# Whole-row loads for the first batch's values, one tile for a group's turned probabilities, uncut products, and a plan with other lengths, in a kernel of banded attention and a gated layer

## The chip, the cores and the metric

The kernel runs on one core of a Trainium2 chip. The metric is the device time of one execution in microseconds (us), the median over several runs. The core's engines are TensorE (PE, the matrix multiplies; the loading of its weights is shown apart, as PEld), VectorE (DVE), ScalarE (ACT), GpSimd (POOL) and SyncE (SP, which here issues the loads from memory). Each engine takes its own instructions strictly in the order in which they were written.

## The reference

```python
# q, k, v: 8 batches x 8 heads x 576 positions x 64; heads 0-3 see the last 32 positions,
# heads 4-7 every fourth of the last 128
scores = scale * np.matmul(q, k.transpose(0, 1, 3, 2))
scores = np.where(masks[None, :, :, :], scores, -1000000000.0)
attn = softmax(scores)                             # written out in the reference
x = heads_side_by_side(np.matmul(attn, v))         # 576 x 512 a batch
h = np.maximum(x @ w_in, 0.0)                      # w_in 512 x 1024
u, v = (h[..., :d_ff // 2], h[..., d_ff // 2:])
v_n = (v - mu) / np.sqrt(var + 1e-06)              # mean and variance over the 512 of a row
v_s = np.einsum('ts,bsd->btd', w_spatial, v_n) + b_spatial[None, :, None]
out = (u * v_s) @ w_out                            # w_out 512 x 512
```

## The kernel before

**Tiles.** The eight heads of a batch are four pairs, and two pairs make a group (`G` = 0 near heads, 1 far heads). The 576 positions are 18 blocks of 32. A block of queries sees 64 keys, its own 32 and the 32 before, and so scores, probabilities and products are many small matmuls, each on a part of TensorE's array. A group's scores come in three units of six blocks (`unit`), each with a maximum, exponentials, a sum, a division on POOL, and a transposition on DVE (L867) that writes the turned probabilities into a tile `pT` of a third of a group. There are four such tiles. `weighted` multiplies a group's values with them, after all three units, into four banks of accumulators: for each block of 32 keys one matmul over the two blocks of queries that see it, 64 columns, but two matmuls of 32 columns where these two lie in different units and so in different tiles. `evacuated` copies the products out and `features_in` splits each pair's into a high and a low part, the features `x` of the layer behind.

Matmuls run at a reduced format, and so every factor is split in two: a copy on ACT (`hi`) and a difference (`lo`), on DVE through `sub` (L537), or by a short fold on TensorE (L600 to L602 for a weight, L651 and L652 for a spatial one) and a copy. A weight's way begins with ACT's first step (L585) and DVE's steps L587, L591 and L594. The gated layer has `v_tile` (the second half of `h`, L973), `upper` (the first half, batch 0), `gate` (the spatial product, L1093) and `piece` (the products with `w_out`, and from batch 1 on those with the first half of `w_in`, as seven products in place of eight, L1281, with sums and differences of factors: `factor`, `joined`).

**Loads.** All loads of keys, values and weights are issued by SyncE into eleven tiles `kqv` of 128 x 1152 numbers. A load takes the tile that its plan gives it and waits on the chip until what stood there has been read. For batch 0 the list `LOADS` sets their order: `kq0` is the keys and queries of a pair (`kq0a` its first third, `kq0b` the rest), `v0` the values of a group, `wi12` a slice of `w_in`, `wo0` of `w_out`, `sp4` of the spatial weights. In memory a key's row holds the 18 blocks' values of both heads of the pair, 4608 bytes in one piece.

**Order.** A planner (`Timeline`) runs while the program is built. Every step is a strand that says, before each part, which engine it needs, for how many microseconds, and which tiles. The planner takes the strand that could start first, corrected by a rank, and writes its instructions. The ranks come from tables (`SHIFT`, `SECOND`, `FIRST`, `RANKS`); the microseconds stand in the code. The chip then keeps this order on each engine, whatever the real lengths. Until 30 us of the plan TensorE's gaps are filled with matmuls on zeros (L1401).

Of the kernel before, what the change touches and what calls it, by code (L numbers as in the profile page):

```python
# [26 lines left out]
    ('differences', 0): 0.468,  # L27
    ('differences', 1): 6.175,
    ('factor', 0): -7.854,
    ('factor', 1): 3.191,  # L30
    ('factor', 10): -9.348,
    ('factor', 11): -10.686,
    ('factor', 12): -7.566,
    ('factor', 13): -0.364,
    ('factor', 14): -3.99,
    ('factor', 2): -2.237,
    ('factor', 3): 1.347,
    ('factor', 4): -5.468,
    ('factor', 5): -2.002,
    ('factor', 6): 0.064,  # L40
    ('factor', 7): 3.683,
    ('factor', 8): -4.426,
    ('factor', 9): 11.423,
    ('features_in', 0): -1.929,
    ('features_in', 1): -6.483,
    ('features_in', 2): 1.799,
    ('features_in', 3): 2.762,
    ('gate', 0): 0.195,
    ('gate', 1): 0.043,
    ('gate', 2): -0.747,  # L50
    ('gate', 3): 3.234,
    ('gate', 4): -0.329,
    ('gate', 5): -3.407,
    ('gate', 6): -5.019,
    ('gate', 7): -2.472,
    ('heads_in', 0): -18.264,
    ('heads_in', 1): -7.458,
    ('heads_in', 2): -11.465,
    ('heads_in', 3): -5.984,
    ('piece', 0): -5.965,  # L60
    ('piece', 1): -2.471,
    ('piece', 10): 1.261,
    ('piece', 11): -3.149,
    ('piece', 12): -0.447,
    ('piece', 13): -1.085,
    ('piece', 14): 0.115,
    ('piece', 15): -6.645,
    ('piece', 16): -3.48,
    ('piece', 17): 0.704,
    ('piece', 18): -3.672,  # L70
    ('piece', 19): -3.913,
    ('piece', 2): -3.945,
    ('piece', 20): 0.716,
    ('piece', 21): 0.502,
    ('piece', 22): -5.774,
    ('piece', 23): -1.128,
    ('piece', 24): -2.828,
    ('piece', 25): -2.689,
    ('piece', 26): 0.874,
    ('piece', 27): 2.135,  # L80
    ('piece', 3): -2.111,
    ('piece', 4): -2.378,
    ('piece', 5): 1.404,
    ('piece', 6): -1.667,
    ('piece', 7): -0.342,
    ('piece', 8): -2.98,
    ('piece', 9): -6.786,
    ('unit', 0): 0.628,
    ('unit', 1): 0.566,
    ('unit', 2): 1.826,  # L90
    ('unit', 3): 0.588,
    ('unit', 4): 0.52,
    ('unit', 5): 0.142,
# [313 lines left out]
def tile_banded_attention_gated_moe(  # L407
# [25 lines left out]
    D = 64  # L433
# [1150 lines left out]
```

## Time and profile before

| | |
|---|---|
| device time, median of 3 runs | 551.05 us (550.04 to 551.29) |
| the profiled execution | 551.94 us, of which its span is 550.2 us |
| TensorE busy | 527.7 us, 7836 instructions |
| DVE busy | 385.4 us, 878 instructions |
| ACT busy | 360.1 us, 970 instructions |
| POOL busy | 194.2 us, 226 instructions |
| moved by DMA | 46.72 MB, mean 85 GB/s |

The span is that of one execution, from its first instruction to its last. Busy times are sums over the whole span, in which stages with different limits follow each other, so what one stage waits for is read from that stage.

### The profile page before, as it was taken

The numbers are of one execution on the slowest core, as the hardware profiler recorded it, in microseconds if no ns is written. First come the engines' busy times: TensorE is split into PE (matmuls) and PEld (weight loads), VectorE is DVE, ScalarE is ACT, GpSimd is POOL, SyncE is SP. The second block draws the span as 40 slices with busy tenths as digits, with TensorE's granted clock in tenths as the row PEclk, the third lists the DMA queues.
The fourth block names the chain that finished last, engine by engine and source line by source line (L and its number), as shares of the span: only waits on it lengthen the run. The fifth ranks groups of instructions, "written<-read, shape, count | busy, mean of one in ns | idle before, by whom it ended". The sixth has DMA issues, their size and how long they took to land.

```text
span 550.2 us, 18561 instructions
## 1 busy us (share of the span) xinstructions
PE 527.7 (96%) x7836; PEld 478.2 (87%) x7836; DVE 385.4 (70%) x878; ACT 360.1 (65%) x970; POOL 194.2 (35%) x226
## 2 busy tenths in 40 slices
PE   9989999995999999999999998899999998999997
PEld 6766798884999979889999998889999998989996
DVE  6864979998867758677669675577758674666554
ACT  4787986756785568745785757746686666646423
POOL 3410337354324522265216341365216440253000
PEclk9998999997999999999999999999999998999999
DMA  8784423203344123221253014221252010001002
GB/s 273 190 306 151 128 69 108 89 4 84 112 130 109 53 79 88 61 72 55 67 143 89 19 60 131 71 72 54 55 142 60 11 66 4 13 0 59 29 1 87
DMA packets 60455, 46.72 MB, mean 85 GB/s; under 512 B 41298, under 2 KB 50514, under 8 KB 60372
## 3 DMA queue, kind: packets, MB, share of 16 engines
q1 hardware_dynamic: 60372, 45.54, 28.2%
q8 instruction: 61, 1.00, 0.8%
q14 instruction: 22, 0.18, 0.1%
HBM read 36.08 MB, written 9.44 MB: 83 GB/s over the span
## 4 chain that ended last, share of the span: by engine, by line
PE 76%; DVE 9%; ACT 6%; DMA 5%; issue 2%; SPq 1%; POOL 0%; DVEq 0%; ACTq 0%
PE bank L1281 31%; PE bank L1093 16%; PE bank L973 12%; PE bank L897 6%; PE bank L797 4%; PE bank L993 2%; DMA kqv<-in_w_in_dram 2%; DMA kqv<-in_w_out_dram 2%; ACT raw L929 2%; PE bank L1073 1%; PE bank L1072 1%; SPq L772 1%; DMA kqv<-in_kT_dram 1%; PE bank L1060 1%; DVE x L537 1%
## 5 line engine op out<-in xcount | busy, mean ns | idle before, releaser
L1093 PE MATMUL bank<-wt,fac 128*128 128x288 f32 x768 | 114.3, 297 | 1.4 <-ACT x L944 1.1
L1093 PEld LDWEIGHTS bank<-wt,fac 128*128 128x128 f32 x768 | 106.6, 189 | 3.2 <-ACT x L944 1.3
L862 POOL TENSOR_TENSOR p<-p,rv 128x384 f32<-128x384 f32 x48 | 42.6, 888 | 123.6 <-DVE rv L860 122.0
L973 PE MATMUL bank<-wih,x 128*128 128x512 f32 x256 | 84.9, 394 | 0.2 <-DVE x L537 0.2
L839 ACT ACTIVATE p<-p,nm 128x64 f32<-128x64 f32 x180 | 60.4, 337 | 10.9 <-DVE nm L833 10.8
L1367 ACT COPY ur<-bank 128x288 f32<-128x288 f32 x120 | 45.7, 397 | 32.4 <-PE bank L1281 28.9
L929 ACT COPY raw<-bank 64x288 f32<-64x288 f32 (+1 forms) x96 | 49.7, 541 | 16.0 <-PE bank L897 14.7
L973 PEld LDWEIGHTS bank<-wih,x 128*128 128x128 f32 x256 | 48.0, 188 | 10.4 <-DVE x L537 0.6
L537 DVE TENSOR_TENSOR fac<-ur,fac 128x576 fp32r<-128x576 f32 x56 | 47.3, 859 | 10.2 <-ACT fac L1210 10.2
L1281 PE MATMUL bank<-fac,woh 128*128 128x288 f32 x256 | 54.1, 302 | 0.0
L1018 POOL TENSOR_TENSOR rs<-rs,halfneg 128x1 f32<-128x1 f32 (+1 forms) x40 | 28.4, 710 | 68.5 <-DVE rs L1015 68.2
L1267 POOL TENSOR_TENSOR raw<-raw,raw 128x576 f32<-128x576 f32 x21 | 33.8, 1608 | 51.6 <-DVE fac L537 40.1
L1210 ACT CAST fac<-ur 128x576 fp32r<-128x576 f32 x56 | 36.7, 673 | 22.9 <-POOL ur L1267 12.5
L1281 PE MATMUL bank<-fac,o 128*128 128x288 f32 x288 | 44.7, 302 | 6.2 <-ACT ur L1367 6.0
L973 PE MATMUL bank<-wil,x 128*128 128x512 f32 x128 | 50.2, 392 | 0.0
L1344 DVE TENSOR_TENSOR ur<-ur,bank 128x288 f32<-128x288 f32 x90 | 39.2, 448 | 14.6 <-PE bank L1281 10.0
L1281 PEld LDWEIGHTS bank<-fac,o 128*128 128x128 f32 x288 | 41.3, 194 | 7.3 <-ACT ur L1367 6.5
L1267 POOL TENSOR_TENSOR ur<-ur,ur 128x576 f32<-128x576 f32 x28 | 41.3, 1475 | 11.8 <-DVE fac L537 8.1
L1281 PEld LDWEIGHTS bank<-fac,woh 128*128 128x128 f32 x256 | 42.8, 193 | 1.9
L897 PE MATMUL bank<-pT,kqv 32*64 32x64 f32 (+1 forms) x2688 | 34.8, 229 | 8.0 <-issue 7.2
L797 PEld LDWEIGHTS bank<-kqv 64*32 64x32 f32 x2304 | 34.8, 119 | 7.3 <-issue 5.9
L897 PEld LDWEIGHTS bank<-pT,kqv 32*64 32x64 f32 x2688 | 32.1, 130 | 10.2 <-issue 8.9
(157 smaller groups left out, 1143.7 us busy)
## 6 DMA issues: line engine op xcount, KB each, us to landing
kqv<-in_vw_dram SPq DMA_DIRECT2D x128, 72.0 KB, 2.6
out_dram<-ur SPq DMA_DIRECT2D x64, 144.0 KB, 1.7
kqv<-in_kT_dram SPq DMA_DIRECT2D x30, 288.0 KB, 3.2
kqv<-in_qT_dram SPq DMA_DIRECT2D x30, 288.0 KB, 4.5
kqv<-in_w_in_dram SPq DMA_DIRECT2D x8, 512.0 KB, 6.7
kqv<-in_w_out_dram SPq DMA_DIRECT2D x4, 512.0 KB
kqv<-in_w_spT_dram SPq DMA_DIRECT2D x5, 288.0 KB, 2.9
kqv<-in_kT_dram SPq DMA_DIRECT2D x2, 192.0 KB, 3.8
```

The lines of the kernel that those rows point to most:

```text
L537: nc.vector.tensor_sub(out, a, b.bitcast(F32))
L797: nc.tensor.matmul(s[w][q * QB : q * QB + QB, e, :], kq[r, :S].rearrange("p (u n i t) -> p u t n i", n=2, i=QB, t=US)[:, (u + places[b, pa ...
L839: nc.scalar.activation(p[:, e, j], s[j][:, e] if first else p[:, e, j], AF.Exp, bias=nm[:, i : i + 1], scale=SCALE if first else 1.0, accu ...
L862: nc.gpsimd.tensor_mul(flat, flat, spread_out(rv))
L897: nc.tensor.matmul(acc[h][i][1][1][col : col + D, o : o + len(run) * QB], v[r, c * D : c * D + D], probs[b, G, u][1][r, at : at + len(run) ...
L929: nc.scalar.copy(dst[to], src[at])
L973: nc.tensor.matmul(pm, x[a][:, cols], wi[w][:, c, NF:], start=c == 0 and n == 0, stop=c == NC - 1 and n == 2)
L1093: nc.tensor.matmul(pv, left[:, a, i, m * P : m * P + P], wt[:, k, h, w, i], start=n == 0, stop=False, skip_group_check=True)
L1267: (eng.tensor_add if kind == "s" and n == 1 else eng.tensor_sub)(at(to), at(left), at(right))
L1281: nc.tensor.matmul(bank[:, :HS], lhs, rhs, start=fresh and n == 0, stop=n == 5, skip_group_check=not fresh or kind == "s")
L1344: nc.vector.tensor_add(ob[1][:, m], ob[1][:, m], bank[:, :HS])
L1367: nc.scalar.copy(ob[1][:, m], bank[:, :HS])
```

## The change

Values of batch 0: a group takes two `kqv` tiles, one for the 32 keys that stand before a block and one for the block's own, and each of its eight loads brings 32 whole rows of 4608 bytes, with both heads of the pair, of which a row's place in the tile uses one. Before, a load brought one head's 18 pieces of 256 bytes from each row, side by side with the other kind's. Later batches load as before. Probabilities: the three transpositions of a group write parts of one tile, of which there are two; the first of them takes the tile, and the others wait until it has. Products: no matmul is cut at a unit's border any more (76 instead of 84 calls a group; the profile counts two instructions for each). The table of masks has 18 places instead of 24, and `minus` has a tile of its own. The planner's lengths for some steps are raised, and the tables of ranks and the list of loads have other numbers throughout.

```diff
-    ('weighted', 0): -3.76,
-    ('weighted', 1): -3.947,
+    ('weighted', 0): -2.858,
+    ('weighted', 1): 1.375,
...
-sp4 kq1b wi00 wi12 kq0a kq0b kq1a kq2 wi11 kq3 wi10 wo0 v0 v1 sp3 wi03 wi02 sp2 sp1 wi13 wi01 wo3 wo1 sp0 wo2
-bias
+kq1a wi11 wi00 wi10 kq0a kq3 wi12 sp1 wi01 bias kq2 kq1b v0 wi13 wi02 wo0 kq0b sp3 v1 sp4 sp2 wo1 wi03 wo3 sp0
+wo2
...
-KNOBS = {'wide': (1, (1, 2)), 'plain': (8, (1, 2))}
+KNOBS = {'apart': 2, 'wide': (1, (1, 2)), 'plain': (8, (1, 2))}
...
-            pT=bufs("pT", [P, 2 * US * KW], 4),
+            pT=bufs("pT", [P, NB * KW], 2),
...
-    masks = const.tile([P, 2 * US + NB, KW], BF16, name="masks")
+    masks = const.tile([P, NB, KW], BF16, name="masks")
...
+        apart = b == 0 and G < KNOBS["apart"]
         yield turn("v", b, G)
-        yield "kqv"
-        (big,) = yield DMA, 4.2, 2.0
-        for i, n in itertools.product(range(2), range(2)):
-            src = vw[b, 2 * G + i, (n + 1) * QB : (n + 2) * QB].rearrange("k (t j d) -> j k t d", j=2, d=D)
-            for j in range(2):
-                to = (2 * i + j) * QB
-                nc.sync.dma_start(big[1][to : to + QB, :BIG].rearrange("p (t n d) -> p t n d", n=2, d=D)[:, :, n, :], src[j])
-        taken("v", b, G, 6.2)
-        values[b, G] = big
+        yield "kqv kqv" if apart else "kqv"
+        got = values[b, G] = yield DMA, 3.8 if apart else 4.8, 2.0
+        for i, n, j in itertools.product(range(2), range(2), range(2)):
+            r = slice((2 * i + j) * QB, (2 * i + j + 1) * QB)
+            src = vw[b, 2 * G + i, (n + 1) * QB : (n + 2) * QB]
+            if apart:
+                nc.sync.dma_start(got[n][1][r], src)
+            else:
+                dst = got[0][1][r].rearrange("p (t n d) -> p t n d", n=2, d=D)
+                nc.sync.dma_start(dst[:, :, n, :], src.rearrange("k (t j d) -> j k t d", j=2, d=D)[j])
+        taken("v", b, G, 5.8 if apart else 6.8)
...
-        *held, pb = yield PE, 0.77 if first else 0.68, 0.0
+        *held, pb = yield PE, 0.8 if first else 0.71, 0.0
...
-        yield "pT"
-        (probs[n],) = yield DVE, 0.5, 0.08
-        nc.vector.transpose(probs[n][1], p.rearrange("p e j k -> p (e j k)"))
+        yield [("turned", b, G)] if u else "pT"
+        got = yield DVE, 0.52, 0.08
+        if u == 0:
+            probs[b, G] = got[0]
+            tl.done("turned", b, G)
+        w = 2 * US * KW
+        nc.vector.transpose(probs[b, G][1][:, u * w : u * w + w], p.rearrange("p e j k -> p (e j k)"))
...
-        got = yield PE, 1.35, 0.0
+        got = yield PE, 1.7, 0.0
...
-        v = values[b, G][1][:, :BIG]
+        v = [x[1].rearrange("p (t c d) -> p t c d", c=2, d=D) for x in values[b, G]]
...
-                split = len({g // (2 * US) for g in to}) > 1
-                runs += [(len([r for r in runs if r[1] == h]) + n, h, c, run) for n, run in enumerate([[g] for g in to] if split else [to])]
+                runs.append((c - h * HB + h, h, c, to))
         for n, h, c, run in sorted(runs):
-            u, k = divmod(run[0], 2 * US)
-            at = (2 * k + (run[0] == c)) * QB
+            at = (2 * run[0] + (run[0] == c)) * QB
...
-                    v[r, c * D : c * D + D],
-                    probs[b, G, u][1][r, at : at + len(run) * QB],
+                    v[c % len(v)][r, c // 2, j if len(v) > 1 else c % 2, :],
+                    probs[b, G][1][r, at : at + len(run) * QB],
...
-        yield DVE2, 0.67, 0.085
+        yield DVE2, 0.78, 0.085
```

How this moves the work is seen in the rows of the programs, in the order in which each engine takes them. First SyncE's queue around the first batch's values, before. A row has the line, the tile that is written (`kqv6_78` is tile 6 of the eleven) and the array it comes from, with the shape of one load and their number.

```order
L753 DMA kqv7_79<-in_kT_dram 128x576
L754 DMA kqv7_79<-in_qT_dram 128x576
L562 DMA kqv8_80<-in_w_in_dram 128x512
L562 DMA kqv9_81<-in_w_out_dram 128x512
L772 DMA kqv10_82<-in_vw_dram 32x9x64 x8
L772 DMA kqv1_73<-in_vw_dram 32x9x64 x8
L630 DMA kqv2_74<-in_w_spT_dram 128x576
L562 DMA kqv3_75<-in_w_in_dram 128x512
L562 DMA kqv4_76<-in_w_in_dram 128x512
L630 DMA kqv6_78<-in_w_spT_dram 128x576
L630 DMA kqv8_80<-in_w_spT_dram 128x576
L562 DMA kqv5_77<-in_w_in_dram 128x512
```

And the same place in the changed program:

```order
L774 DMA kqv4_76<-in_vw_dram 32x1152 x2
L774 DMA kqv0_72<-in_vw_dram 32x1152 x2
L774 DMA kqv4_76<-in_vw_dram 32x1152 x2
L774 DMA kqv0_72<-in_vw_dram 32x1152 x2
L631 DMA kqv8_80<-in_w_spT_dram 128x576
L631 DMA kqv9_81<-in_w_spT_dram 128x576
L774 DMA kqv10_82<-in_vw_dram 32x1152 x2
L774 DMA kqv5_77<-in_vw_dram 32x1152 x2
L774 DMA kqv10_82<-in_vw_dram 32x1152 x2
L774 DMA kqv5_77<-in_vw_dram 32x1152 x2
L563 DMA kqv1_73<-in_w_out_dram 128x512
L563 DMA kqv4_76<-in_w_in_dram 128x512
```

Before, four slices of `w_in` were issued ahead of the values, the last of them here into tile 8, and four behind them (tiles 3, 4, 5 and 7); the values went to tile 10, which was free, and to tile 1. Now seven slices stand ahead, only one behind (tile 4), and the first group's values go to tiles 4 and 0, in which the keys and queries of that group stood, the second's to 10 and 5, those of its own keys.

Second, TensorE behind the products of the second group: the last of these, then folds of weights, and the first rows of `v_tile` (L973 before, L978 in the changed program). Before:

```order
L897 MATMUL bank5_69<-pT2_90,kqv1_73 64x32 x2
L897 MATMUL bank2_66<-pT2_90,kqv1_73 64x32 x2
L651 MATMUL bank0_64<-kqv6_78,plus_126 128x288
L652 MATMUL bank0_64<-wt_139,wd_127 128x288
L600 MATMUL bank3_67<-kqv4_76,plus_126 128x512
L601 MATMUL bank3_67<-wih_135,wd_127 128x512
L602 MATMUL bank3_67<-wil_136,plus_126 128x512
L651 MATMUL bank1_65<-kqv8_80,plus_126 128x288
L652 MATMUL bank1_65<-wt_139,wd_127 128x288
L973 MATMUL bank6_70<-wih_135,x0_143 128x512
L973 MATMUL bank6_70<-wil_136,x0_143 128x512
L973 MATMUL bank6_70<-wih_135,x0_143 128x512 x2
```

And in the changed program:

```order
L904 MATMUL bank0_64<-pT1_89,kqv10_82 64x64 x2
L904 MATMUL bank4_68<-pT1_89,kqv10_82 64x64 x2
L904 MATMUL bank0_64<-pT1_89,kqv5_77 64x32 x2
L904 MATMUL bank4_68<-pT1_89,kqv5_77 64x32 x2
L601 MATMUL bank7_71<-kqv2_74,plus_124 128x512
L602 MATMUL bank7_71<-wih_133,minus_125 128x512
L603 MATMUL bank7_71<-wil_134,plus_124 128x512
L978 MATMUL bank1_65<-wih_133,x0_141 128x512
L978 MATMUL bank1_65<-wil_134,x0_141 128x512
```

The two spatial folds (L651 and L652) that stood between the second products and `v_tile` have gone ahead of the products, and one fold of a slice of `w_in` (L600 to L602) stands there, as before. Further down, behind the first rows of `v_tile`, two more folds of `w_in` stood before and one stands now (beside one of `w_out`), so that one of these has gone ahead as well.

Third, TensorE at the first group's scores (L797 before, L801 now; `bank1_65` is one of eight banks) and the filler (L1401 before, L1406 now). In the changed program the second unit to be scored is of the second group, and the filler stands around it:

```order
L801 MATMUL bank3_67<-kqv4_76 32x64 x2
L801 MATMUL bank3_67<-kqv0_72 32x64 x2
L801 MATMUL bank4_68<-kqv4_76 32x64 x2
L801 MATMUL bank4_68<-kqv0_72 32x64 x2
L1406 MATMUL bank0_64<-fac3_100 128x512 x18
L801 MATMUL bank5_69<-kqv10_82 32x64 x2
L801 MATMUL bank5_69<-kqv5_77 32x64 x2
L801 MATMUL bank6_70<-kqv10_82 32x64 x2
L801 MATMUL bank6_70<-kqv5_77 32x64 x2
```

In the program before, five instructions of filler stand between the first group's first two units:

```order
L797 MATMUL bank2_66<-kqv4_76 32x64 x2
L797 MATMUL bank3_67<-kqv3_75 32x64 x2
L797 MATMUL bank3_67<-kqv4_76 32x64 x2
L1401 MATMUL bank0_64<-fac3_102 128x512 x5
L791 LDWEIGHTS room_105
L791 MATMUL bank4_68<-room_105 128x64
```

The filler between the first two units has grown from 5 to 18 instructions, and the unit behind it is one of the other group.

## Rows read from the trace of the kernel before

**Rows 1.** The page's part 1: engine, busy us, share of span, instructions.

```profile
PE 527.7 (96%) x7836; PEld 478.2 (87%) x7836; DVE 385.4 (70%) x878; ACT 360.1 (65%) x970; POOL 194.2 (35%) x226
```

**Rows 2.** Windows: stretch, its length, each engine's busy us (instructions), PEclk, DMA share, GB/s.

```profile
0.00:131.58 131.58, 119.94 (x1934) 97.16 (x1935) 104.15 (x249) 93.16 (x267) 51.60 (x70) 0.98 0.48 142
12.00:60.00 48.00, 44.38 (x761) 32.13 (x761) 31.75 (x79) 37.66 (x106) 9.74 (x12) 0.96 0.69 207
36.00:48.00 12.00, 10.02 (x191) 6.82 (x192) 5.62 (x12) 8.75 (x17) 0.00 (x0) 0.86 0.69 241
120.00:132.00 12.00, 5.97 (x32) 4.78 (x32) 11.69 (x24) 5.16 (x11) 7.24 (x8) 0.87 0.22 49
240.00:252.00 12.00, 12.00 (x70) 10.51 (x70) 7.38 (x19) 7.09 (x12) 7.28 (x9) 1.00 0.01 1
```

**Rows 3.** Waits of TensorE: waiter <- waited for: total us, times, longest us.

```profile
PE bank L897 <- issue: 7.2, 4, 2.1
PE bank L1281 <- ACT ur L1367: 6.0, 1, 6.0
PE bank L1281 <- ACT raw L929: 1.5, 1, 1.5
PE bank L1093 <- ACT x L944: 1.1, 1, 1.1
```

**Rows 4.** Timeline of TensorE: start, us, line, out<-in, shapes, count [idle before].

```profile
38.66 1.92 PE L897 MATMUL bank<-pT,kqv 32*64 32x64 f32 x158
...
51.95 1.06 PE L600 MATMUL bank<-kqv,plus 128*128 128x512 f32 x2
...
53.31 1.06 PE L600 MATMUL bank<-kqv,plus 128*128 128x512 f32 x2
...
131.58 3.25 PE L1281 MATMUL bank<-fac,o 128*128 128x288 f32 x12 [6.03 <-ACT ur L1367]
...
160.74 2.02 PE L897 MATMUL bank<-pT,kqv 32*64 32x64 f32 x168
```

**Rows 5.** Timeline of DVE, at the fourth feature and at the factor differences.

```profile
53.58 0.76 DVE L537 TENSOR_TENSOR x<-raw,x 128x576 fp32r<-128x576 f32 x1 [1.06 <-ACT x L944]
...
128.03 3.74 DVE L537 TENSOR_TENSOR fac<-ur,fac 128x576 fp32r<-128x576 f32 x3
```

**Rows 6.** Waits of all engines in the first 54 us.

```profile
DVE kqv L587 <- ACT kqv L585: 9.5, 4, 5.4
ACT kqv L585 <- DMA kqv<-in_w_in_dram: 9.2, 5, 3.2
```

**Rows 7.** Timeline of SyncE's queue of loads: a weight, then the values.

```profile
10.31 0.43 SPq L562 DMA_DIRECT2D kqv<-in_w_in_dram  x1
...
11.45 16.07 SPq L772 DMA_DIRECT2D kqv<-in_vw_dram  x16
```

**Rows 8.** Windows of the first 40 us, columns as in rows 2.

```profile
0.00:20.00 20.00, 18.96 (x214) 13.95 (x215) 13.05 (x40) 9.48 (x25) 5.80 (x19) 1.00 0.92 283
20.00:28.00 8.00, 6.70 (x263) 5.20 (x262) 7.11 (x20) 7.25 (x39) 4.87 (x6) 1.00 0.44 94
32.00:40.00 8.00, 7.67 (x150) 5.00 (x153) 4.58 (x12) 6.01 (x12) 0.83 (x1) 1.00 1.00 384
```

**Rows 9.** Groups of DVE by line and shape: count | busy us, mean ns.

```profile
L587 DVE TENSOR_SCALAR kqv<-kqv 128x512 uint32<-128x512 uint32 x12 | 5.1, 422 | 9.5 <-ACT kqv L585 9.5
...
L594 DVE SCALAR_TENSOR_TENSOR wil<-kqv,ur 128x512 fp32r<-128x512 uint32 x6 | 4.2, 692 | 0.2
...
L537 DVE TENSOR_TENSOR wt<-kqv,wt 128x576 fp32r<-128x576 f32 x2 | 1.5, 751 | 0.0
```

**Rows 10.** Groups of TensorE by line and shape: scores, then products.

```profile
L797 PE MATMUL bank<-kqv 64*32 64x64 f32 x2304 | 40.5, 219 | 0.0
...
L897 PE MATMUL bank<-pT,kqv 32*64 32x64 f32 x1792 | 32.9, 233 | 3.9 <-issue 3.3 <-DVE pT L867 0.6
L897 PE MATMUL bank<-pT,kqv 32*64 32x32 f32 x896 | 27.4, 220 | 4.1 <-issue 3.9
```

More of the change, by code (lines that the diff above doesn't have):

```diff
@@ L26 @@
 SHIFT = {
[L27 to L44, printed above, removed]
@@ L101 @@
-    ('weighted', 0): -3.76,
-    ('weighted', 1): -3.947,
+    ('differences', 0): 3.922,
+    ('differences', 1): 2.198,
+    ('factor', 0): -10.234,
+    ('factor', 1): 1.385,
+    ('factor', 10): -11.435,
+    ('factor', 11): -5.549,
+    ('factor', 12): -15.936,
+    ('factor', 13): -1.457,
+    ('factor', 14): -1.612,
+    ('factor', 2): -3.581,
+    ('factor', 3): -14.055,
+    ('factor', 4): -5.141,
+    ('factor', 5): 2.382,
+    ('factor', 6): -6.88,
+    ('factor', 7): 1.211,
+    ('factor', 8): 0.771,
@@ new lines @@
+    ('piece', 27): 4.573,
+    ('piece', 3): 0.443,
+    ('piece', 4): 0.154,
+    ('piece', 5): 3.95,
+    ('piece', 6): -2.039,
+    ('piece', 7): -3.342,
+    ('piece', 8): -0.708,
+    ('piece', 9): -1.811,
+    ('unit', 0): 0.804,
+    ('unit', 1): 1.043,
+    ('unit', 2): 3.593,
+    ('unit', 3): 1.151,
+    ('unit', 4): 1.207,
+    ('unit', 5): 0.681,
+    ('v_tile', 0): -1.79,
+    ('v_tile', 1): 1.488,
+    ('v_tile', 2): -0.169,
+    ('v_tile', 3): -1.063,
+    ('v_tile', 4): -3.863,
@@ new lines @@
+    ('piece', 20): -11.229,
+    ('piece', 21): -3.172,
+    ('piece', 22): -24.594,
+    ('piece', 23): -8.921,
+    ('piece', 24): -1.791,
+    ('piece', 25): -5.281,
+    ('piece', 26): -10.316,
+    ('piece', 27): -6.568,
+    ('piece', 3): -0.461,
+    ('piece', 4): 4.085,
+    ('piece', 5): -13.715,
+    ('piece', 6): 0.067,
+    ('piece', 7): 0.276,
+    ('piece', 8): 4.999,
+    ('piece', 9): 2.894,
+    ('unit', 0): -1.764,
+    ('unit', 1): -2.555,
+    ('unit', 2): -4.758,
+    ('unit', 3): 1.341,
@@ new lines @@
+    ('piece', 10): 3.988,
+    ('piece', 11): -17.128,
+    ('piece', 12): -3.293,
+    ('piece', 13): -2.622,
+    ('piece', 2): -5.702,
+    ('piece', 3): -11.192,
+    ('piece', 4): 0.089,
+    ('piece', 5): 0.75,
+    ('piece', 6): 3.542,
+    ('piece', 7): -16.637,
+    ('piece', 8): 2.946,
+    ('piece', 9): -4.367,
+    ('unit', 0): -4.818,
+    ('unit', 1): -7.185,
+    ('unit', 2): -11.016,
+    ('unit', 3): -2.657,
+    ('unit', 4): -1.539,
+    ('unit', 5): -0.527,
+    ('upper', 0): -16.557,
@@ L905, in weighted @@
         tl.done("weighted", b, G)
-        for u in range(NU):
-            tl.give(probs[b, G, u])
-        tl.give(values[b, G])
+        tl.give(probs[b, G], *values[b, G])
         for h, i in itertools.product(range(2), range(2)):
```

401 lines of the change are left out of this document (174 added, 227 removed).

## The prediction

> **What bounds the kernel now.** I read the engines' busy time first: TensorE works 96% of the span, DVE 70% [rows 1]. TensorE bounds the whole, then, but only where nothing holds it up, so the question is where its 22 us of idle time lie. The table of 12 us stretches answers: from 240 us on (one batch stands for all) TensorE fills its stretch at full clock, and it falls back most between 36 and 48 and between 120 and 132 us [rows 2]. The list of its waits names them: 7.2 us in four places inside the products of probabilities and values (L897), where nothing that the profile shows is waited for, and one of 6.0 us in the output products (L1281), put down to ACT [rows 3]. That second one ends at 131.58 [rows 4]. Just before it DVE writes three factor differences back to back, from 128.03 on [rows 5], in a stretch in which DVE is busy 11.69 of 12 us: TensorE waits for DVE, which is late. [...]
>
> Why is DVE late? Not for the length of its list alone. Before 54 us it sits idle for long: 9.5 us in four waits for ACT's first step on a weight (L585), and ACT in turn waits 9.2 us in five places for weights from memory [rows 6]. So I went to the queue of loads. SyncE issues everything in order. From 11.45 to 27.52 us it issues the 16 loads of the first batch's values, 1.0 us each, and only then goes on to the rest of the weights [rows 7]. From 20 to 28 us the DMA engines move 94 GB/s; from 32 to 40 us, with long rows, 384 [rows 8]. The stage that sets the change's worth is the first 54 us, and what it delays shows at 131.58.
>
> **The change part by part.** *Values as whole rows.* Each of a group's 8 loads becomes 32 rows of 4608 bytes, where it was 288 pieces of 256. No row of before shows such a load; the nearest is a weight's (128 rows of 4 KB), whose issue takes 0.43 us [rows 7]. 16 issues cost 7 us of SyncE then, for 16. Twice the bytes are moved: 1.18 MB more, at 384 GB/s 3.1 us more of transfer [rows 8]. Against this stands the hole from 20 to 28 us, in which 0.75 MB moved where 3.07 could have: 6.0 us. The values' net is 2.9 us earlier for what lies behind them. Bounds: 3.1 us later, if the hole has another cause, and 6 us earlier.
>
> *The new order of loads* puts seven of eight input weights ahead of the values. It also binds the values to the keys: both value tiles of group 0 reuse the buffers of its keys, so their loads wait for the third score unit of group 0, which TensorE now runs behind 18 more filler matmuls. By the bytes ahead of them and the rates of [rows 8] the last third of those keys lands at about 19 us, that unit ends at about 25, the first group's values land at about 30 and the second's at about 35.
>
> *What the engines make of it.* I walked the first 85 rows of DVE and the first 66 of ACT in the new order, each with the mean length of its group and from the landings above. DVE's sixth transposition ends at about 38 (two weights and a bias difference stand ahead of it that stood behind, one feature fewer). The second group's products run from about 39.1 to 41 (before from 38.66 [rows 4]), held by the first group's evacuations until then, the evacuations and casts follow on ACT, and the fourth feature is ready at about 51.4. Before it starts at 53.58 [rows 5] and is copied out by 54.6: 3.2 us gained. By then DVE has done one weight more (0.42 + 0.42 + 0.69 us) and two differences of the spatial weights more (0.75 each), less small things 2.7 us net [rows 9]. From there to the tenth factor difference, the last of the three before 131.58, the two lists hold the same kinds of work (by the groups' means 101.2 us of DVE from the start in the old order, where the trace itself has 104.15 [rows 2], and 101.4 in the new). So DVE reaches it 3.2 + 2.7 = **5.9 us** earlier, at about 125.5. TensorE is there in time: it waited 6.0 us, has less to do after the second products (one weight's fold, 1.36 us from one start to the next [rows 4], and two shorter spatial ones went ahead of them), and is behind the features by no more than they are. Bounds: 0, if DVE gets other waits in return, and 13, if all but 3 us of its idle time from 12 to 60 us goes (16.2 us: 48 less its busy time [rows 2]).
>
> *Uncut products.* The matmuls per group fall from 168 to 152 recorded instructions, and the columns streamed stay equal, since 32 instructions of 32 columns become 16 of 64. A group takes 2.02 us when undisturbed [rows 4]. If time goes by instructions, 16 x 12.0 ns = 0.19 us a group is gained, 3.1 us over 16; if by columns, nothing. Score units, all of 64 columns, take 40.5 us for 2304 instructions, 17.6 ns each, which speaks for columns; that an instruction of 32 columns is recorded with 220 ns and one of 64 with 233 speaks for instructions [rows 10]. I take the middle, **1.6 us**. [...]
>
> *Probabilities of a group in one tile* (two such, for four of a third of a group): products waited for all three thirds anyway, and a transposition found a free tile in this trace: TensorE's only wait for one is 0.6 us [rows 10]. Nothing, unless a group's tile comes free late, which would hold DVE's list, and all behind it, for up to a group's products, 2.02 us. *Masks* in one step fewer and the separate identity: under 0.1 us of DVE, in its idle start.
>
> *The new numbers for the later batches* move pieces by one or two places. The waits left there, up to 2.1 us inside each of two groups of products, 1.5 and 1.1 us [rows 3], I carry over unchanged; all gone would be up to 6.8 us, doubled as much on the other side.
>
> *Sum:* 5.9 + 1.6 = 7.5 us. The profiled execution took 551.94 us, 1.74 over its span and 0.9 above the median of 551.05; off the median this gives **543.5 us**.
>
> **The rivals.** *Products only.* DVE's list is as long as before, and what it saves in loads it loses by head-of-line waits: the new order puts a unit of group 1, whose keys land at 17 us, ahead of a weight that is there at 15. For it: every engine runs strictly in order, and 5.4 of DVE's 9.5 us came in a single wait [rows 6]. Then 551.05 - 1.6 = 549.5. *The later batches take it back.* Four more waits inside products, as four of the sixteen groups have them now, cost 7.2 us again [rows 3]: 550.7, no change. Against it: the stretch of 240 to 252 us is filled to the end [rows 2]. [...] *More than that:* all DVE waits for weights go, the stall at 125 vanishes with its clock loss, and two later waits with it: 538.
>
> **How the numbers follow.** Forecast 0.50 (539.5 to 547.5), products only 0.14, taken back 0.13, bytes bind 0.10, more 0.13. Under 0.2% (1.1 us) this kernel's change can't be told from none. Faster: 0.50 + 0.13 + most of products only, 0.12, and 0.05 of taken back: 0.80. Same: 0.09. Slower: 0.11. For 8 in 10 the range reaches down to 537 and up to 551, which takes in products only and the easier half of taken back.
>
> **What would show it.** In the new trace: SyncE's value loads under 0.5 us each, apart from their wait for buffers; over 300 GB/s in 20 to 35 us; the fourth feature at 50 to 53 us; the wait before the factor pieces near 125 us ended some 6 us earlier; a group of products at 1.8 to 2.0 us. The prediction is wrong if the fourth feature comes after 54 us, if TensorE idles more than 6 us between the first products and the first feature, or if new waits stand in the batches after 140 us.

## The result, and the profile after

The changed kernel takes 544.09 us (median of 4, 543.51 to 544.69), the kernel before 551.17: a ratio of 0.987 (95% interval 0.985 to 0.989). The forecast was 543.5 us, 7.5 us of gain against 7.1 measured. The profiled execution took 543.74 us with a span of 542.0, 8.2 us shorter than before. The number was right. The larger of its two terms was right in size and place, but not for the reason given, as the experiments below show.

The page's first part, which answers to [rows 1], and from its part on queues the line of TensorE's own instructions:

```profile
PE 524.1 (97%) x7572; PEld 472.3 (87%) x7572; DVE 392.1 (72%) x877; ACT 358.6 (66%) x970; POOL 193.2 (36%) x226
...
q8 instruction: 59, 0.97, 0.8%
```

TensorE does 264 matmuls less (256 by the uncut products, 8 of filler) and is idle 17.9 us instead of 22.5. Windows of the changed kernel, columns as in [rows 2], with one stretch more:

```profile
36.00:48.00 12.00, 10.93 (x303) 7.95 (x304) 7.36 (x17) 9.11 (x19) 1.66 (x2) 0.86 1.02 285
120.00:132.00 12.00, 10.48 (x139) 8.14 (x138) 11.69 (x27) 9.51 (x28) 6.33 (x8) 1.00 0.38 96
192.00:204.00 12.00, 9.82 (x186) 7.59 (x188) 4.07 (x11) 6.76 (x15) 3.19 (x6) 0.86 0.20 66
240.00:252.00 12.00, 12.00 (x80) 11.29 (x78) 9.25 (x21) 8.87 (x15) 4.05 (x7) 1.00 0.04 14
```

From 120 to 132 us TensorE is now busy 10.48 us instead of 5.97, at a granted clock of 1.00 instead of 0.87. From 36 to 48 us little has changed, and the clock is the same 0.86. New is a poor stretch from 192 to 204 us, where before nothing was lost. TensorE's waits in the changed kernel, which answer to [rows 3]:

```profile
PE bank L904 <- issue: 4.3, 5, 2.2
PE bank L801 <- issue: 1.2, 3, 0.6
...
PE bank L904 <- DMA kqv<-in_vw_dram: 1.0, 3, 0.4
...
PE bank L1286 <- DVE fac L537: 0.7, 1, 0.7
```

The wait of 6.0 us in the output products is down to 0.7, with a wait for DVE of 0.8 us some 3 us ahead of it (shown with the experiments); the waits for nothing that the profile shows ("issue") are still there, in other places. TensorE's timeline, second products, output products, the wait in the new poor stretch, and a group of products that nothing disturbs:

```profile
43.58 1.63 PE L904 MATMUL bank<-pT,kqv 32*64 32x64 f32 x130 [0.27 <-DMA kqv<-in_vw_dram]
...
128.94 1.74 PE L1286 MATMUL bank<-fac,o 128*128 128x288 f32 x11 [0.72 <-DVE fac L537]
...
197.78 0.24 PE L904 MATMUL bank<-pT,kqv 32*64 32x32 f32 x2 [2.18 <-issue]
...
218.12 1.89 PE L904 MATMUL bank<-pT,kqv 32*64 32x64 f32 x152
```

The output products no longer wait 6.03 but 0.72 us. Their first matmul starts at 127.94, the others follow from 128.94; before, the first started at 131.58 [rows 4]. An undisturbed group takes 1.89 instead of 2.02 us. DVE at the fourth feature and at the eighth to tenth factor differences, as in [rows 5]:

```profile
52.85 0.75 DVE L537 TENSOR_TENSOR x<-raw,x 128x576 fp32r<-128x576 f32 x1
...
126.47 1.42 DVE L537 TENSOR_TENSOR fac<-ur,fac 128x576 fp32r<-128x576 f32 x2
...
128.14 0.75 DVE L537 TENSOR_TENSOR fac<-ur,fac 128x576 fp32r<-128x576 f32 x1
```

The fourth feature starts only 0.7 us earlier (52.85 for 53.58), the tenth difference ends 2.9 us earlier (128.89 for 131.77). Last the loads: SyncE's queue at the values, its longest wait there, and windows of the DMA engines, as in [rows 7, 8]:

```profile
27.60 3.98 SPq L774 DMA_DIRECT2D kqv<-in_vw_dram  x8
...
33.49 5.22 SPq L774 DMA_DIRECT2D kqv<-in_vw_dram  x8
...
SPq L774 <- PE bank L801: 7.4, 1, 7.4
```

```profile
20.00:28.00 8.00, 6.89 (x121) 5.11 (x122) 6.51 (x21) 7.54 (x32) 2.63 (x4) 1.00 0.43 153
28.00:32.00 4.00, 4.00 (x77) 2.28 (x79) 3.83 (x11) 3.97 (x18) 0.00 (x0) 1.00 0.86 212
32.00:40.00 8.00, 6.58 (x208) 5.21 (x197) 7.17 (x18) 5.16 (x20) 3.33 (x4) 0.90 1.03 240
```

A whole-row load took 0.50 us to issue in the first group and 0.65 in the second, where 0.43 were forecast and a load in pieces had taken 1.0. But the values were issued no earlier than 27.60 us, after 7.4 us of waiting for the scores that read their tiles. From 20 to 28 us only 153 GB/s moved, and in the windows in which the values ran 212 to 240, with the DMA engines 86% busy and more, not the 384 of before.

### The profile page after: what moved, and what is told of

It is laid out like the page before. It is cut to its first block, busy times and chain, and to the rows that moved or that the text cites. A ratio compares the mean times of both kernels' runs of the same rounds, so it can differ in the third digit from the quotient of the medians.

```text
span 542.0 us, 18039 instructions
## 1 busy us (share of the span) xinstructions
PE 524.1 (97%) x7572; PEld 472.3 (87%) x7572; DVE 392.1 (72%) x877; ACT 358.6 (66%) x970; POOL 193.2 (36%) x226
## 4 chain that ended last, share of the span: by engine, by line
PE 87%; ACT 4%; DMA 3%; DVE 3%; issue 2%; SPq 0%; ACTq 0%
PE bank L1286 31%; PE bank L1098 19%; PE bank L978 15%; PE bank L801 7%; PE bank L904 5%; PE bank L998 2%; PE bank L1065 2%; PE bank L1406 2%; PE bank L1078 2%; ACT raw L934 2%; PE bank L1077 2%; DMA kqv<-in_w_in_dram 1%; PE bank L601 1%; DMA kqv<-in_vw_dram 1%; DMA kqv<-in_w_out_dram 1%
## 5 line engine op out<-in xcount | busy, mean ns | idle before, releaser
L978 PE MATMUL bank<-wih,x 128*128 128x512 f32 x256 | 89.4, 402 | 1.6 <-DVE p L836 0.8
L537 DVE TENSOR_TENSOR fac<-ur,fac 128x576 fp32r<-128x576 f32 x56 | 52.8, 957 | 18.4 <-ACT fac L1215 18.0
L978 PEld LDWEIGHTS bank<-wih,x 128*128 128x128 f32 x256 | 48.9, 191 | 13.3 <-DVE p L836 1.2
L1349 DVE TENSOR_TENSOR ur<-ur,bank 128x288 f32<-128x288 f32 x90 | 40.1, 448 | 23.2 <-ACT ur L1372 9.0
L1286 PE MATMUL bank<-fac,woh 128*128 128x288 f32 x256 | 52.3, 295 | 0.6 <-ACT ur L1372 0.5
L978 PE MATMUL bank<-wil,x 128*128 128x512 f32 x128 | 50.9, 398 | 0.0
L1272 POOL TENSOR_TENSOR raw<-raw,raw 128x576 f32<-128x576 f32 x21 | 32.1, 1529 | 39.7 <-DVE fac L537 34.2
L1023 POOL TENSOR_TENSOR rs<-rs,halfneg 128x1 f32<-128x1 f32 (+1 forms) x40 | 25.2, 629 | 56.6 <-DVE rs L1020 56.4
L801 PEld LDWEIGHTS bank<-kqv 64*32 64x32 f32 x2304 | 35.8, 119 | 10.0 <-issue 7.6
L1286 PE MATMUL bank<-fac,o 128*128 128x288 f32 x288 | 43.6, 295 | 0.9 <-DVE fac L537 0.7
L801 PE MATMUL bank<-kqv 64*32 64x64 f32 x2304 | 42.7, 219 | 1.2 <-issue 1.2
L1286 PEld LDWEIGHTS bank<-fac,o 128*128 128x128 f32 x288 | 40.2, 188 | 2.2 <-DVE fac L537 1.1
L537 DVE TENSOR_TENSOR fac<-mid,fac 128x512 fp32r<-128x512 f32 x32 | 25.3, 793 | 18.2 <-ACT fac L1215 18.1
```

Of the source, the lines that this page charges most:

```text
L537: nc.vector.tensor_sub(out, a, b.bitcast(F32))
L801: nc.tensor.matmul(s[w][q * QB : q * QB + QB, e, :], kq[r, :S].rearrange("p (u n i t) -> p u t n i", n=2, i=QB, t=US)[:, (u + places[b, pa ...
L978: nc.tensor.matmul(pm, x[a][:, cols], wi[w][:, c, NF:], start=c == 0 and n == 0, stop=c == NC - 1 and n == 2)
L1272: (eng.tensor_add if kind == "s" and n == 1 else eng.tensor_sub)(at(to), at(left), at(right))
L1286: nc.tensor.matmul(bank[:, :HS], lhs, rhs, start=fresh and n == 0, stop=n == 5, skip_group_check=not fresh or kind == "s")
L1349: nc.vector.tensor_add(ob[1][:, m], ob[1][:, m], bank[:, :HS])
```

## Where the time came from

The table below is not the profiler's: it is worked out from the records of TensorE's matmuls. Each matmul counts by the time that usually lies between it and the next at full clock (a group of products 1.90 us, filler nothing), and the columns say by how much a kernel has done the same work earlier than the kernel before (us; minus is later). The last five are kernels of the experiments.

```
work  before at | after  pieces   cut   shift128 | bef.early bef.late
  20     48.55  |   1.5     2.5  -4.7    -16.0   |    0.4     -0.4
  60     89.77  |   1.0     2.5  -5.4    -15.2   |    0.2     -1.8
  90    121.55  |  -0.2     1.6  -7.5    -16.0   |    0.2     -0.6
 100    139.88  |   5.6     7.3  -2.2    -10.4   |    0.2     -0.1
 148    189.61  |   5.0     5.7  -3.9    -11.9   |    0.0     -0.3
 172    214.45  |   1.5     4.2  -3.5    -13.0   |    0.1     -0.6
 304    354.77  |   5.9     8.5  -1.7     -9.1   |    0.4      0.4
 412    468.43  |   8.0    10.5   1.1     -6.4   |    2.7      2.4
 489    546.12  |   7.3     9.8   0.2     -7.1   |    2.4      2.1
```

Up to 90 us of work the changed kernel gains nothing: what it leads by at 60 it has lost again. At the stall it gains 5.8 us at once, of which a part is the granted clock: 0.50 of full speed from 130 to 134 us in the kernel before, 1.00 in the changed one. Then it loses 3.5 us at one wait of 2.18 us and the lower clock behind it (0.72 granted from 198 to 200 us, 0.50 from 200 to 202), and wins 6.5 where the kernel before waits (at 225, 338 to 349 and 462 us).

## The experiments

Each was timed in five rounds beside the kernel before. Theory A is the prediction's: the values' load brings DVE ahead, and this ends the stall.

**Pieces again, in the new order.**

```diff
-            if apart:
-                nc.sync.dma_start(got[n][1][r], src)
-            else:
+            if True:
                 dst = got[0][1][r].rearrange("p (t n d) -> p t n d", n=2, d=D)
...
-        v = [x[1].rearrange("p (t c d) -> p t c d", c=2, d=D) for x in values[b, G]]
+        v = [x[1].rearrange("p (t c d) -> p t c d", c=2, d=D) for x in values[b, G][:1]]
```

> The changed kernel with its order, tiles and plan kept, only the first batch's values again loaded as pieces of 256 bytes (16 loads, into one of the two tiles that a group takes). Theory A (the rows' shorter issue and transfer make the features come earlier, and this feeds DVE's lead at the first output products): 16 issues of 1.0 us each behind the same wait for buffers, second group's values landing some 3 to 5 us later, fourth feature at about 56 instead of 53 us, time 546 to 548. Rival B (the order of loads and the ranks made the gain, the rows nothing): 544, within 0.5 of the changed kernel.

Measured: 543.42 us, ratio 0.984 (0.979 to 0.989), no slower than with whole rows. The queue of loads, windows of the DMA engines, and DVE's fourth feature in this kernel:

```profile
27.07 6.04 SPq L775 DMA_DIRECT2D kqv<-in_vw_dram  x8
...
34.33 5.81 SPq L775 DMA_DIRECT2D kqv<-in_vw_dram  x8
```

```profile
28.00:32.00 4.00, 4.00 (x105) 2.55 (x103) 3.83 (x11) 3.97 (x18) 0.00 (x0) 1.00 0.47 99
32.00:40.00 8.00, 6.91 (x172) 4.91 (x169) 6.98 (x16) 5.89 (x22) 3.33 (x4) 1.00 0.62 156
```

```profile
52.30 0.75 DVE L537 TENSOR_TENSOR x<-raw,x 128x576 fp32r<-128x576 f32 x1
```

A load in pieces took 0.74 us here, so both values were issued by 40.1 us, against 38.7 with whole rows. But they carry half the bytes: the DMA engines were 47 to 62% busy, not full. The fourth feature starts at 52.30, 0.55 us earlier than with whole rows. Theory A's first step falls, and Rival B stands: in this order, rows instead of pieces gave nothing.

**Products cut again, in the new order.**

```diff
-                runs.append((c - h * HB + h, h, c, to))
+                split = len({g // (2 * US) for g in to}) > 1
+                runs += [(len([r for r in runs if r[1] == h]) + n, h, c, run)
+                         for n, run in enumerate([[g] for g in to] if split else [to])]
```

> The changed kernel with the order kept, only the products cut at the units' borders again (168 instead of 152 recorded matmuls a group). If time goes by instructions, an undisturbed group takes 2.0 instead of 1.88 us and the whole 546.2 (16 x 0.13 us more); if by columns, 544. Theory C (waits inside instruction-dense stretches come at every 256th instruction of TensorE, where the next block of instructions has not landed): the waits move to other places too, since each group now holds 32 instructions more, and their sum changes by up to some 3 us either way; by the spacing of the blocks about 1 us less, so 545.

Measured: 550.34 us, ratio 0.998 (0.996 to 1.001); 6.2 us slower than uncut, more than any of the forecasts. TensorE's timeline in it, inside the second products and at an undisturbed group:

```profile
49.16 0.64 PE L905 MATMUL bank<-pT,kqv 32*64 32x64 f32 x12 [3.62 <-issue]
...
287.12 2.02 PE L905 MATMUL bank<-pT,kqv 32*64 32x64 f32 x168
```

The undisturbed group takes 2.02 us again, so its time does go by instructions: 0.13 us a group, 2.1 us in all. Most of the rest is one wait of 3.62 us inside the second products and the lower clock after it (0.78 granted from 48 to 60 us): the column "cut" stands 4.7 us behind at 20, where the changed kernel leads by 1.5.

**Where these waits come from.** I counted all of TensorE's instructions in the trace in the order of their starts, from 0: matmuls, weight loads, and the semaphore and drain instructions between them, without which the count drifts. All but the shortest waits put down to "issue", and two that the profile puts down to ACT [rows 3], stand before an instruction whose number is 193 plus a multiple of 256 (or before the matmul whose weight load has that number):

```
waits at instruction 193 + 256 n (time: us)                                    sum
before    28: 1.30   43: 1.98  225: 1.07  338: 1.49  349: 2.15  462: 1.78        9.8
after     24: 1.11   74: 0.67  103: 1.15  146: 0.37  198: 2.18  276: 0.57
         336: 0.44  396: 0.22  404: 0.51  455: 0.60                              7.8
cut       24: 0.83   49: 3.62   92: 1.27  109: 1.46  159: 1.36  226: 1.23
         282: 0.21  342: 0.82  404: 0.48                                        11.3
shift92  162: 1.77  286: 1.84  350: 0.66  411: 0.79                              5.1
shift128 119: 0.88  163: 0.91  171: 0.14  214: 1.42  291: 1.39  419: 0.26
         470: 0.63                                                               5.6
```

The page counts 61 packets on the queue of TensorE's instructions for the kernel before, and 59 (above) for the changed one:

```profile
q8 instruction: 61, 1.00, 0.8%
```

These are 1.00 MB and 0.97 MB, 16.4 KB each, and 15743 and 15202 counted instructions make 61.5 and 59.4 blocks of 256, one packet for each whole block. Three blocks that ran in 1.36, 1.45 and 1.48 us were followed by gaps, from start to start, of 2.4, 2.2 and 2.4. It isn't a fixed price: other blocks of 1.45 and 1.48 us were followed by gaps of 0.9 and 0.8, and one of 1.34 us by none.

The times of the queue's packets in the traces tell what sets it. Taken in order, each packet lands ahead of one such boundary (the first packet ahead of the second boundary, and so on). In the five kernels of the table no boundary is crossed less than 1.2 us after its packet landed, and every wait listed ends 1.2 to 1.6 us after: a packet that landed at 347.07 in the kernel before stands ahead of the wait that ends at 348.55, one at 196.36 in the changed kernel ahead of the one that ends at 197.78. The block of 1.34 us began at 218.15, and the packet for the boundary behind it had landed at 217.50. So I take it that TensorE waits there for its next block of instructions.

**The count moved, by 92 and by 128 matmuls more in the filler.** The edit for 92; for 128 the limits are 42 and 44:

```diff
-            nc.tensor.matmul(got[0][1]..., z, z.unsqueeze(1).broadcast_to([P, 4, P]), ...)
+            wide = got[0][1].rearrange("p (n c) -> p n c", n=4)
+            parts = 4 if count < 30 else 2 if count < 32 else 1
+            for n in range(0, 4, 4 // parts):
+                nc.tensor.matmul(wide[:, n : n + 4 // parts], z, ...)
+            count += 1
```

> The changed kernel with 92 more matmuls of filler in the first 25 us, made by splitting 512 columns into four times 128, so that no column is added: only the count of TensorE's instructions before everything else rises by 184 (a weight load and a matmul each). Theory C: the waits of 0.4 to 2.2 us now at instructions 193 + 256 n, eleven of them, move, and at the new places the 256 instructions before rarely run in under 3.5 us; of some 10 us of such waits 3 to 4 are left, the lower clock after the wait at 196 us goes too, and the time is 536 to 539. Rival D (these waits belong to the groups of products themselves, to a buffer or a semaphore that the profile does not show): they stay where they are and the time stays at 544 within 0.5.

> The control to the run with 92: 128 more matmuls of filler by the same splitting, 256 instructions more, one whole block. Theory C: the waits stand at the same work as in the changed kernel (the third-to-last matmul of a group of products at 198 us, a score unit at 276, and so on) and the time is 543.5 to 545. If not the count but the finer filler itself did something in the run with 92, this run shows it too: 536 to 539.

Measured: 555.19 us (ratio 1.006, 1.004 to 1.008) and 560.21 us (1.014, 1.009 to 1.018). As times both missed, since the finer filler isn't free. TensorE's first row with 92 more, and in the changed kernel:

```profile
1.04 20.74 PE L1410 MATMUL bank<-fac 128*128 128x128 f32 x96 [1.04 <-DVE fac L484]
```

```profile
1.04 7.29 PE L1406 MATMUL bank<-fac 128*128 128x512 f32 x24 [1.04 <-DVE fac L484]
```

96 matmuls of 128 columns took 20.74 us where 24 of 512 took 7.29. So everything began some 14 us later. As a test of places they hold: with 256 instructions more, six waits stand 15 to 17 us later at the same work (119 for 103, 163 for 146, 214 for 198, 291 for 276, 419 for 404, 470 for 455). The other four of the changed kernel are not there: a boundary need not bring a wait, and of that kernel's 59 only ten have one in the table. With 184 more, none stands at the work where the changed kernel has its long ones. Theory C holds for the places, Rival D falls; the times that were forecast from it did not come. A second thing is seen in the run with 128, at its output products:

```profile
145.05 1.73 PE L1286 MATMUL bank<-fac,o 128*128 128x288 f32 x11 [0.72 <-DVE fac L537]
```

All starts 16 us later, and still the stall of 6 us isn't there.

**The count moved at a small price**, with eight fillers replaced by twelve small matmuls each:

```diff
+            small = 12 if count % 3 == 2 and count < 24 else 0
+            for n in range(small):
+                q, r = n % 4 * QB, slice(n % 2 * D, n % 2 * D + D)
+                nc.tensor.matmul(got[0][1][q : q + QB, ...], ident0[r, :QB], ident0[r, :KW], ...)
```

> The run with 92 added 13 us of filler time at the start, so it tested the places of the waits and not their price. Here eight of the first 24 fillers (before 10 us, when TensorE waits for weights anyway) are each replaced by twelve matmuls of 32 x 64, like those of a score unit, which ran at 17.6 ns each: 88 matmuls, 176 instructions more, and no longer time at the start. Theory C: the waits at instructions 193 + 256 n leave the places of the changed kernel (198, 104, 25 us and so on) for ones at about 142, 265, 275 and 325 us; of 7.8 us some 3 are left, with the lower clock behind 198 us gone too: 537 to 540. Rival: what goes in one place comes in another, time within 1 us of 544.

Measured: 547.3 us, ratio 0.992 (0.989 to 0.996), no faster than the changed kernel and outside both forecasts. The profile counts two matmuls for each of the small ones, so the count rose by 368 instructions, and not by the 176 expected: the places that were expected were not tested. The long waits did leave their places, but two came inside the first batch's products:

```profile
42.44 0.21 PE L904 MATMUL bank<-pT,kqv 32*64 32x32 f32 x1 [2.80 <-issue]
...
50.90 0.65 PE L904 MATMUL bank<-pT,kqv 32*64 32x64 f32 x36 [1.93 <-issue]
```

Waits at 256th instructions sum to 10.2 us here. The prices I could not forecast: in the table's kernels a wait ends 1.2 to 1.6 us after its packet landed, and I had no forecast of the landings.

**DVE later, in the changed kernel.** One reduction of 3.34 us more, at two places:

```diff
+        if b == 0 and hp == 3:
+            nc.vector.tensor_reduce(late, plus.bitcast(F32).unsqueeze(1).broadcast_to([P, 24, P]), axis=AX.X, op=ALU.max)
...
+        if kind == "o" and i == 1:
+            nc.vector.tensor_reduce(late, plus.bitcast(F32).unsqueeze(1).broadcast_to([P, 24, P]), axis=AX.X, op=ALU.max)
```

> The changed kernel with one more DVE instruction of about 3 us (a maximum over a broadcast tile, its result unused) right behind the fourth feature, at 54 us; TensorE's count is the same. The prediction's step (what DVE gains or loses by 54 us it keeps in full until the tenth factor difference): that difference comes 3 us later, the wait at 129 us grows from 0.7 to some 3.7, and the time is 546.5 to 548. Rival E (DVE waits for others between 74 and 84 us, 4.6 us idle, and so forgets what it gained at 54): the time stays within 0.7 of 544.

> The same 3 us of DVE work behind a sum of output weights, at about 100 us, after DVE's idle time. If DVE's lateness sets the wait before the first output products, the tenth factor difference comes 2 to 3 us later (DVE is idle 2 us between 96 and 120), the wait at 129 us grows by as much and the time is 545.5 to 548. If these products wait for something else, the time stays at 544.

Measured: 546.0 us (ratio 0.990, 0.987 to 0.994) and 544.76 us (0.989, 0.986 to 0.993). DVE's added row and TensorE's output products, first with the early one, then with the late one:

```profile
53.74 3.34 DVE L957 TENSOR_REDUCE late<-plus 128x24 f32<-128x3072 f32 x1
...
130.33 1.73 PE L1289 MATMUL bank<-fac,o 128*128 128x288 f32 x11 [0.72 <-DVE fac L538]
```

```profile
103.40 3.34 DVE L1181 TENSOR_REDUCE late<-plus 128x24 f32<-128x3072 f32 x1
...
130.46 1.73 PE L1289 MATMUL bank<-fac,o 128*128 128x288 f32 x11 [0.72 <-DVE fac L538]
```

The wait stays at 0.72 us in both, and neither time can be told from the changed kernel's; the early one's 546.0 lies between what Rival E gave (within 0.7 of 544) and what the step gave (546.5 to 548). The 0.72 alone proves little, since TensorE has waited for DVE just before it, and from there on the two run the same rows. In the changed kernel:

```profile
125.75 0.50 PE L978 MATMUL bank<-wih,x 128*128 128x512 f32 x1 [0.80 <-DVE p L836]
```

This earlier wait is 0.81 us with the early reduction; with the late one it is 1.03, and a new one of 0.52 stands ahead of it. What counts is how far TensorE falls behind: its output products go on 1.39 and 1.52 us later than the changed kernel's, and part of that was lost before the reduction. By the records TensorE with the early one is 0.9 us behind the changed kernel at 40 us of work, 1.6 at 45 and 1.5 at 100: of 3.34 us it has kept 0.7 at most. So Rival E holds for the early place. The late one cost 0.9 us up to 100 us of work, a quarter of what was put in.

**DVE earlier, in the kernel before.**

```diff
-        nc.vector.bn_stats(st[:m], vr[:m])
+        nc.vector.bn_stats(st[:m], vr[:m, : 32 if b == 0 else NF])
```

```diff
-        sub(xl, src, xh)
+        few = slice(0, 64 if b == 1 else S)
+        sub(xl[:, few], src[:, few], xh[:, few])
```

> The kernel before, its order on every engine kept, with less DVE work early: the five statistics of the first batch (55 to 75 us) are taken over 32 columns in place of 512, some 0.57 us less for each, 2.9 us together; the first batch's means and variances are those of 32 columns. The prediction's step (what DVE gains early shows in full at the stall that ends at 131.58): the stall is 3 us shorter, 548. Rival E (DVE waits for others between 72 and 84 us and gives it back): stall 6 us as before, 551 within 0.7.

> The kernel before, order kept, with less DVE work late: the low parts of the second batch's four features (84 to 126 us) are written over 64 columns in place of 576, some 0.6 us less for each, 2.4 us together; the rest of the second batch's low parts stays that of the first. If DVE's list between 84 us and the tenth factor difference is what makes TensorE wait, the stall is 2 to 2.5 us shorter and the time 548 to 549.5, the clock's share with it. [...]

Measured: 549.72 us (ratio 0.998, 0.994 to 1.001) and 550.14 us (0.998, 0.995 to 1.001), no difference that can be told. The stall in the first and in the second:

```profile
131.49 3.25 PE L1281 MATMUL bank<-fac,o 128*128 128x288 f32 x12 [6.03 <-ACT ur L1367]
```

```profile
131.38 3.25 PE L1282 MATMUL bank<-fac,o 128*128 128x288 f32 x12 [5.52 <-ACT ur L1368]
```

In the first the five statistics, between 57 and 76 us, took 0.15 to 0.19 us instead of 0.65 to 0.69: with 2.5 us less DVE work the stall is 6.03 us, the same to the hundredth. Theory A's second step falls too: what DVE gains in the early stage doesn't reach the stall. The second says less. Of its four differences, between 87 and 110 us, three took 0.2 us instead of 0.7, but the last one ran beside a sum on POOL and took longer than the whole one's 0.74:

```profile
108.21 1.31 DVE L537 TENSOR_TENSOR x<-raw,x 128x64 fp32r<-128x64 f32 x1
```

So only 1.0 us of DVE work was taken away, not the 2.4 expected, and the stall is 5.52.

**Parts undone or done alone, with the planner free to make its order again.** Three kernels: the changed code with the first batch's tables of before, the changed kernel with `'apart': 0`, and the kernel before with group tiles and uncut products.

> The changed code (whole rows, group tiles, uncut products, its lengths, its numbers for the later batches) with the first batch's ranks, the weights' ranks and the list of loads of the kernel before. If the new order of the first batch and of the loads removed the stall at 131 us, it is back: a wait of 4 to 6 us before the first output products, 549 to 552. If the whole rows or the numbers of the second batch did it, 543 to 546. The waits of Theory C move too, by up to 2 us in either sense.

> The changed kernel with the first batch's values loaded as before, in pieces and into one tile a group; ranks, lengths, list of loads and all else as changed; the planner makes its order again, which moves a few rows on each engine. After the run with pieces in the same order, which lost nothing: 541 to 545. If the rows are worth what the prediction gave them, 547 or more. It is also a candidate for the fastest version, since a group takes one tile less.

> The kernel before with its numbers, lengths and loads, but with a group's turned probabilities in one tile (two such), the products uncut, and the masks' table and the negative identity as changed; the planner makes its order again, most rows staying. By the instructions saved, 0.13 us a group over 16 groups, 2.1 us: 549. The stall at 131 us stays (5 to 6 us). Theory C adds up to 3 us of waits in either sense: 546 to 552.

Measured: 577.97, 568.54 and 605.49 us (ratios 1.048, 1.031 and 1.098, each to within 0.005). All far outside what any theory gave. TensorE's longest waits in the second and the third:

```profile
PE bank L1286 <- DVE fac L537: 6.6, 2, 6.4
PE bank L602 <- ACT woh L625: 5.7, 1, 5.7
```

```profile
PE bank L1283 <- DVE p L833: 11.9, 3, 6.2
PE bank L1283 <- DVE fac L537: 11.5, 10, 2.1
PE bank L1283 <- ACT fac L1212: 10.6, 2, 7.8
```

New waits for DVE and ACT appear all along. These runs don't price the part that they undo; they show that tables, lengths and steps were fitted to each other. The pieces in the kept order cost nothing, the same pieces in an order made anew 24 us.

## Why the prediction was right, and where it wasn't

**Values as rows** ("2.9 us earlier for what lies behind them"): wrong. The rate of 384 GB/s came from loads over 128 rows; in the windows of these over 32 rows it was 212 to 240, and the wait for tiles (7.4 us) took what the faster issue saved. The pieces in the same order did as well. Of the rivals "bytes bind" (0.10), by which the doubled bytes delay what lies behind them, was nearer: the second group's last wait for values ended at 43.58, where they were forecast to land at about 35. But the price did not come: the fourth feature starts 0.7 us earlier than before, and the granted clock from 36 to 48 us is 0.86 as before.

**The fourth feature** (3.2 us): 0.7 us.

**"DVE reaches it 5.9 us earlier":** 2.9 us, and the step that failed is the one under it, that what DVE gains by 54 us shows in full at the tenth factor difference. Both directions were tried: 3.34 us added in the changed kernel and 2.5 us taken away before left the wait as it was. Between 72 and 84 us DVE is idle 4.6 us (3.5 before), 2.6 us of it in one wait for ACT (2.0 before).

**The stall:** forecast 5.9 us gained, measured 5.8. That the two agree is luck, since the lead that was added up came only in small part. The changed kernel and the three others of the table in the new order gain 5.3 to 5.8 us there, also the one that runs 16 us later, with rows or pieces, with products cut or not; less DVE work early does nothing to it in the old order. So it is the new order itself that ends the stall, not what it does to DVE's early lead.

The trace of before shows why, and the prediction misread it in one point. TensorE doesn't wait for the tenth difference, which ends at 131.77, behind the start of the output products at 131.58. It waits for a copy on ACT, which waited for the ninth (ended at 131.09). And TensorE had waited for DVE once more, at 109.73:

```profile
109.73 0.73 PE L973 MATMUL bank<-wih,x 128*128 128x512 f32 x2 [0.17 <-DVE x L537]
...
131.13 0.40 ACT L1367 COPY ur<-bank 128x288 f32<-128x288 f32 x1 [1.91 <-DVE fac L537]
```

At 109.73 the two engines stand level, whatever came before. From there DVE has rows until 131.09 and is idle only 0.9 us; TensorE has 15.8 us of work, and the rest is its wait. With less DVE work early they stand level at 109.64, the same rows follow, and so does the same wait. What shortens it has to change DVE's rows behind this place. The new order does: from the second batch's fourth feature (ended at 109.67 before, 111.83 after) to the end of the tenth difference DVE takes 22.1 us before and 17.1 after. Among the rows that have left this stretch are one factor difference, three differences of output weights (`wol` and two of `o`), a transposition and the statistics of the last 64 positions; two differences of `u` have come. POOL has a part in it: before, the second of the three differences in [rows 5] ran beside a sum on POOL and took 1.95 us, where one alone takes 0.75; in the changed program these sums come earlier, and the last three differences take 0.75 each. No run moves these rows alone, so what each of them is worth stays open. The group tiles were not undone in a kept order either. POOL's timeline before, and after:

```profile
125.67 1.40 POOL L1267 TENSOR_TENSOR ur<-ur,ur 128x576 f32<-128x576 f32 x1
...
128.57 1.91 POOL L1267 TENSOR_TENSOR ur<-ur,ur 128x576 f32<-128x576 f32 x1
```

```profile
121.61 1.43 POOL L1272 TENSOR_TENSOR ur<-ur,ur 128x576 f32<-128x576 f32 x1
...
123.78 1.43 POOL L1272 TENSOR_TENSOR ur<-ur,ur 128x576 f32<-128x576 f32 x1
```

**Uncut products** (1.6 us, the middle of 0 and 3.1): by the undisturbed groups 2.1 us. Uncutting also moves every later boundary of TensorE's blocks; put back in the same order, the cuts cost 6.2 us, of which one wait of 3.62 us at a boundary and the clock behind it (0.78 granted from 48 to 60 us) took the larger part.

**"The waits left there ... I carry over unchanged":** wrong. All six of before are gone and ten others have come, for 2.0 us less. New waits after 140 us were one of the prediction's own signs that it is wrong, and they came. From 100 us of work to the end the lead grows by 1.7 us where 1.2 was forecast. That the sum came out is in part luck of places.

## What to carry to other kernels

A stall put down to a late engine says nothing of how far back its lateness can be cured: look for the last place ahead of it where the waiting engine already waited for the late one, or the late one was idle, since here what was gained before that place was given back in it. Test it by adding and removing a few microseconds of work in the kept order, and check in the trace that the work really got shorter. Where a planner's tables are fitted to the code, keep the order when a part is undone; a new plan with unfitted numbers cost 24 to 54 us here. On TensorE, look whether waits without a releaser stand a fixed number of instructions apart (256 here), and when the packets of the instruction queue landed. The edits here that put 32 a group, 184 or 368 instructions more ahead moved such waits, and with the first two their sum went either way, from 7.8 us to 11.3 and to 5.1.

## What the runs showed of the hardware that was not expected

TensorE's waits at 256th instructions, up to 3.62 us each, 9.8 us in the kernel before and 7.8 in the changed one; each ended 1.2 to 1.6 us after a packet of its instruction queue had landed. In the filler at the start, full-array matmuls of 128 columns with their own weights took 216 ns each on average over 96, those of 512 columns 304 over 24. In the windows in which loads of 32 rows of 4608 bytes ran, 212 to 240 GB/s were moved with the DMA engines 86% busy and more; loads in pieces of 256 bytes took 0.74 us each to issue, and the engines were 47 to 62% busy. A DVE difference of 64 columns took 1.31 us beside a sum on POOL, and 0.2 us without one.
